# A new order table for a gated recurrence and an FFT gate on one core

## The chip, the core and the metric

The kernel runs on one core of one Trainium2 chip. The core has five engines that run side by side, each with its own queue of instructions in a fixed order: TensorE (PE in the profile, with its weight loads as PEld), VectorE (DVE), ScalarE (ACT), GpSimd (POOL) and SyncE (SP), which issues all DMA transfers of this kernel. The metric is the device time of one execution in microseconds (us), lower is better.

## The reference, cut to what matters

For four batches of 6272 tokens with 256 channels, a gated recurrence over time is followed by a gate with a convolution over the whole sequence, done by an FFT:

```
sig = 1 / (1 + exp(-f_logit))
f = lower_bound + (1 - lower_bound) * sig;  i = 1 - f
for t in range(S): h = f[:, t] * h + i[:, t] * x[:, t];  y[:, t] = h      # y is the next x
proj = x @ w_proj;  x1, x2, x3 = the three thirds of proj
x2_conv = irfft(rfft(x2, axis=1) * rfft(filter_fft, axis=0), axis=1)
out = (x1 * x2_conv * x3) @ w_out
```

## The kernel before

**The work of one batch**, in the names that the text uses (the operation's name in the program, its line in the profile):

- The recurrence goes in 13 chunks of 512 tokens (chunk 12 has 128). For a chunk, SP issues two loads of 512 KB (L331): the logit into FL and x into XT. `sig` is the sigmoid on ACT, in place in FL (L334). `u` multiplies XT by FL on POOL (L336). `su` turns FL and XT on PE into PSUM, once for each half of the channels, "a" and "b" (L348, 16 transposes each: eight of FL, eight of XT). `f` (L361 on ACT or L363 on DVE) and `scan` (DVE, L369) make the state, and `wrap` copies some of it (POOL L292, or ACT). FL and XT have three slots each, so the loads of chunk c wait until `su` b of chunk c-3 has read the slot. In batch 0 there are some slots more.
- Phase P (PE, L703) is the x2 projection, in 13 groups of which one is short; each is copied out of PSUM by ACT or DVE (`x2`, L280 or L285, tile X). It needs all scans of the batch. Then come the stages of the FFT: F1 (L716) with its copies, and 16 units of F2 (L778), of the product with the filter's spectrum (`prod`: DVE straight from PSUM, L801, or a copy by ACT or DVE and then `pm` on POOL, L810), of I2 (L820) and of the copy `Th`. A small product for each unit (`slot`, POOL L783) precedes I2. SP loads a unit's spectrum, H, from DRAM (L756), where the filter's stage at the start has stored it (`hst`, L660).
- `x13` (PE, L397) projects x1 and x3, and their product becomes zt (`xs`, `z`).
- Phase O has 13 groups: I1 (PE, L883), `y` (DVE, L889, tile ys, two buffers), `proj` (PE, L901), `o` (the copy out of PSUM, mostly ACT, L282 into osb, PP or HA) and `store` (SP, L913).

Phase O of one batch runs beside the recurrence of the next: while PE does I1 and proj of batch 0, it does `su` of batch 1 between them.

**The order.** Every operation is declared once, with its reads and writes, in a list (`Plan.op`); nothing is issued then. The string `ORDER` holds one word of three characters for each of the 2419 operations: the operation's number, its engine (with "MUL" for a product that DVE takes straight from PSUM), and for what PE writes, the PSUM bank. `emit` goes through the string and issues the operations in its order, and the waits between engines follow from the data. So the string fixes three things: each engine's queue (SP's too), who does an operation that two engines can do, and the PSUM banks, of which there are eight; most of PE's operations take a pair.

```
def order(self):
    ...
    for at in range(0, len(ORDER), 3):
        a, b, c = (value[d] for d in ORDER[at:at + 3])
        word = a * 4096 + b * 64 + c
        yield word // 64, self.ENGINES[word // 8 % 8], word % 8
```

An engine that comes to an operation whose data aren't there waits, with all that stands behind it in its queue. For SP that means that a load stands behind a store that waits for its copy.

Of the kernel before, what the change touches and what calls it, by code (L numbers as in the profile page):

```python
# [61 lines left out]
class Plan:  # L62
# [63 lines left out]
    "A3gA7gAzgA/gAAYAOYAVIA0YA4AAhQAcQABIACIAPIASYAQAAWIAjQAaQAbQAdQAfQAgQAeQA5QA1SAoUBAYAiUA2KA8ABHgBfgBPgAlUBBUArWAnWBD"  # L126
    "gBLgBXgBTgBbgBjgA9WAsSA6ABIYBJSBCMBEYAyAARAAYUAwVDqgDrgDngAkVD2gECgADgD3gDpgEOgDogEDgEPgEagAqVBQIA+OAXIBFQAmVBRWAuVB"
    "SGApVBGAAZEBKKBYIAUIBMYBNSATYBUYAxVBZWBgABOKBaOAtVBVQBWABcIAvUBhWBiOBdUBkYBeEBlQBmIBpUBqMBwQBxIBnWBoODsAD4ADtYEEAB3U"
    "BuQBvIBrYAEYByYBsWBtOB4EDuSBzQB+UB0AB5WD5YDyQB/EB6GCAUEQACBEDvKDwKB7YEFYCCYB8SDzID0ID6WB9CCDUCEED+QCJSCQUD/AEcAEmgD7"
    "OD8OERYEbgCKKCRMCOWEAIEngEygEGSCHUCIMCPGEHCEIKEoAEdYCLYCSYEKWCTQELGCMUCUACNEEMOESSCZQETKCXWE0AEWUCaICYGCeQCgWEUKE8gE"  # L130
    "zgAFgE9gFGgFQgCGgEpYEJYCbYEXMEYME+ACfAChGCcSCdCEeQEiWEjGEfIEgICnUCoECpSEqUEkOAIACqCCjQCwSCuWErECiYE1YAJYCkAEsMEuQFIA"
    "CvGCsUCxKE2SCzWEvIEwICtEC+UC0GE3KE4KE5QCrYAHYAKYCyYC/EE/YE6ADAWE7IDBGC3UFASC5WFSAC4EDDQC6GFDUDEAC8WC9GEhYFHgFbgF6gFJ"
    "YCVgFRgCmgC7YFTYDCYFagCFgFkgFlgB2gFugCWgDGgFvgAGgFcAFBKFCKFKSDJQJTWJUXFEMFFMFLKDKAJWHJVODOUDPEFmAFMKDHQFNWDIAJYUFOOF"
    "POJaEFUSDQQFVCDRADMUFWKFXWFdYDNEFwAFnYDLYEtYALYDSYAMYEVYElYFxYDXQFYOFZOFeSDYADTUFfCFhQDUEDZWFgKFiADaGFjIFoUFpEDeSDfC"
    "DgWDhGFrQFySDcWFqMJZUJdVFzKF0KF1SFsAMugB1gC2gF4gGlgG3gF/gDWgClgDFgMigMWgF5gC1gMXgD1YEBYExYJXYANYDxYD9YDbYF7YF8YDiYFt"
    "IF2KF3KDdGDjWJbsJeQJiRENAEZAJfFGHSGTUJkBJgoDkOGVQGJWGWIGICMwAGUEGKOGXSGFQGZUGYCGGIGaEMkAGBWGRSGDUGSCGLQGNSGCOMYAGEMG"
    "MIGOKGPUGQEJjWJnXJoQJluJpHJqoGbUDmgDlgHAgMjgDVgGugGdSGhWGcEGeKGfQGmUJsSGiGGgAGosGqsF9WJuCJtTHTgHJQJxSJvrF+GGjUJzCGvW"
    "GkMHKAG4SHLUG8CG6CGrYMZYGxuGzuGnYGwYGpYGsQG5YJyWJ2SJ3TG9YG0YG7YGyYGtAHMEG1QHBUG2AJ0uJ4KJ5rHFsHDsHPWHNQJ7TJ8SKAVHQGG+"
    "WKBUJ9DHOAJ+qHRQHUSKCNHSIG/GHYCMlYHWqKFVKGQKHFKIoKDsHVYHCYHGYHEYHHWHcgMvgGAgHlgHdSHfqHhqHIGHmQH3WHZYKEYHqAHXYHaUHgYH"
    "eYHrYHooHpYHiYHnYH4GHbEKKSKLRKMCKNBH5WHjUH7SH6OHvQHugIBgHkEH8CH9UH+EHsWHzoHxoICSHtGH/UIAMIEqIGCKPRMaWKRBJwYHwYH0YMxY"  # L140
    "JcYHyYKOYIFYILUMbGMeQIPEIHYIDYMcOMfAH1SKQVH2CMgIKStIKgINsITgIcgM6gIvgIlWImGIISIJCIdQIfAIUWIWGIYuIhAMmSMqUIQYIZYIVYIM"
    "YJmYIOYIXYI4gM7gNGgNHgJBgMrEMnKMsMMoKKUWKWGIRQKVXKZWISAKXvIaQIwUI0sIiYIgYIeYM8AM9YI1YMdYIbAKbGInSIpQKaXKeWKfVKcvIysI"
    "oCIqAIrSKjXKgGIsCKlPIjQKkUKhtIkAKmsItSI5WIuKNIAMyQM2UMzAI7uI9GM0INSgJKgKoSKpTKtWKuXNTgKqCKrrKnYIxYKJYJrYNJYJhYIzYM3E"
    "M4MM+QKvGKwHI2SM/ANCWI3CNAIJCUKySKzTNKQJGsNDGJEENegNEOK0CK1rNOUK3SNUANLAJ/YKsYK2YI+YI8YI6YKdYKxYKTYJHYJ6YKYYJFYNVYI/"
    "WK5CNPENMIJAGK4TK8SK9QLBRJLWK+CNgAJPGNQMK6rLDBNWUNaSNXELCRK/oLGQJNuNbCNYMNfgNogNpgLEpLIANqAJOYNzgNygLFYJ1YJMYJDYLAYN"
    "hYJQYKiYJIWLHQLJoJJGNiULLRLMQNlWNcKNjENkMJRSLOALNBNmGLQRLRQRyUJSCRzVLaSNnOLSBLToK7YNrYLKYLPYLUYLbKR0ER1FLVWNsQNvUNtA"
    "N0ANwELWOLcSNuILXWNxMLdCLkQLlILfSLYGLgKN9gN8gNRYNNYN1YNZYN+AN/YN2UN5WN3EN6GLmQLhSN4MN7OLuULvMOHgOGgLnALiCOIALpQOAWOD"
    "SLwULqILrQOECOFKOBGOCOL4SL5KLxELZgOQgLegLogORgLsAOSAOJYM5YM1YMhYMtYOKULzQONWObgOagLjgOTYNBYNFYOLEOOGL6SL7CL0IL1QL2AO"
    "MMOPOL9UL+MOUSOXQOVCR3WR4XOYAOcAL/UOWKOdYNdYOZIR5GR6HMpYOeSOhWU1gVBgL3gLygVOgVNgOfCOgKLtgOiGMAEMBgU2gVCgL8gMHQMCSOjO"
    "O4WU3AO5GMDKMIIOyUOmSOzEOnCO8QOuWO9IO2UOqQO3EOrIOkSO0UVDAOlCO1EOvOOwQOoSOxIOpCOsUVPAOtMO6QO7AMESMMUMNMMFCPAQPEWO+SPC"  # L150
    "UPBAO/KMJQMRSPFGPDEMGgMKAPIWMSKPGUPQSPHMPUCPoQPMuPKuMOUVEYU4YPNYPLYR2YR8XPJYR9TR+PPSqPpAPOQPYWPcuPauPdYPbYPTYPRYPVYM"
    "PER/DPPAPgUPsQPkEPtAPWSSBXSCVPZYR7YSDPSEtPisPlYPjYPhYSAYPXCPqQPrAPeSPuWPzQPfCPygP3oP1oMLgP7gQEgQNgPvGSGVSHUSIFSJEPmS"
    "P8WPnCPwUSLRSNBP+GU5SSMQPxMQAuSOoQBYP2YSKYP4YU6CQWUP0YP9YP/YP5WQXEU7KU9QP6GQFUQOSQJEU+IU/IQSCQCWQQqSQVSRTSSFSTrQaQSV"
    "VSWSQDGQHsSXNQIYQKYQGYQTYQRYQYWQbAQZGSaTQcQSbUSfWSgVScDSYqSZYShOSdsQdAQLSQeWQfOQggQpgQygQ7gVZgVagQhQSiFQMCQlAQjoVFUQ"
# [830 lines left out]
```

## Time and profile before

| what | value |
|---|---|
| median of 3 runs | 455.66 us (455.5 to 456.23) |
| the profiled execution's own time | 457.66 us |
| its span, first to last instruction | 455.5 us |
| busy PE, DVE, ACT, POOL | 96%, 90%, 86%, 68% of the span |
| granted TensorE clock | 0.998 |
| DMA | 119.04 MB, mean 261 GB/s |

The span is what the trace shows; 2.16 us of the profiled execution lie around it. A busy PE is not PE at its peak, because its matmuls overlap and their ends are modelled. In rows of the timeline the first number is the start in us, the second the length of the stretch, and brackets at the end give the engine's idle time before it and what ended that.

### The profile page before, as it was taken

The numbers are of one execution on the slowest core, as the hardware profiler recorded it, in microseconds if no ns is written. First come the engines' busy times: TensorE is split into PE (matmuls) and PEld (weight loads), VectorE is DVE, ScalarE is ACT, GpSimd is POOL, SyncE is SP. The second block draws the span as 40 slices with busy tenths as digits, with TensorE's granted clock in tenths as the row PEclk, the third lists the DMA queues.
The fourth block names the chain that finished last, engine by engine and source line by source line (L and its number), as shares of the span: only waits on it lengthen the run. The fifth ranks groups of instructions, "written<-read, shape, count | busy, mean of one in ns | idle before, by whom it ended". The sixth has DMA issues, their size and how long they took to land.

```text
span 455.5 us, 14537 instructions
## 1 busy us (share of the span) xinstructions
PE 436.8 (96%) x6017; PEld 344.1 (76%) x6017; DVE 407.9 (90%) x456; ACT 392.8 (86%) x545; POOL 307.6 (68%) x287
## 2 busy tenths in 40 slices
PE   8999999999999999999999999999999899999994
PEld 6877778667767889767768988776769797776783
DVE  5889998899999986999999987999999859988973
ACT  5789998889999988999988978999999778998354
POOL 4588994289998642889986626999996505657300
PEclk9999999999999999999999999999999999999999
DMA  8999979767797977559956893589586822763167
GB/s 326 406 402 380 373 254 362 275 217 242 273 322 237 333 250 316 173 172 325 357 195 232 308 358 146 179 293 339 192 309 210 349 115 89 219 199 111 47 266 302
DMA packets 42562, 119.04 MB, mean 261 GB/s; under 512 B 4096, under 2 KB 5760, under 8 KB 42496
## 3 DMA queue, kind: packets, MB, share of 16 engines
q1 hardware_dynamic: 42496, 118.11, 72.7%
q8 instruction: 47, 0.77, 0.7%
q14 instruction: 19, 0.16, 0.1%
HBM read 86.12 MB, written 31.98 MB: 259 GB/s over the span
## 4 chain that ended last, share of the span: by engine, by line
PE 58%; DVE 14%; ACT 8%; issue 5%; DMA 5%; POOL 3%; SPq 0%; DVEq 0%; ACTq 0%; POOLq 0%
PE PS L397 14%; PE PS L820 8%; PE PS L703 7%; PE PS L901 7%; DVE HA L369 6%; PE PS L348 6%; PE PS L716 5%; PE PS L778 5%; DMA FL<-in_f_logit_dram 3%; PE PS L883 3%; DVE ys L889 3%; DMA XT<-in_x_dram 2%; DVE fTs L363 2%; PE PS L633 2%; DVE PP L801 2%
## 5 line engine op out<-in xcount | busy, mean ns | idle before, releaser
L336 POOL TENSOR_TENSOR XT<-XT,FL 128x1024 f32<-128x1024 f32 (+1 forms) x47 | 105.1, 2239 | 59.5 <-ACT FL L334 31.7
L369 DVE TENSOR_TENSOR_SCAN HA<-fTs,HA,PS 128x512 f16<-128x512 f32 (+1 forms) x96 | 112.8, 1204 | 3.0 <-ACT fTs L361 2.2
L397 PE MATMUL PS<-HA,W 128*128 128x490 f16 (+1 forms) x416 | 100.4, 367 | 0.3 <-ACT XS L282 0.2
L810 POOL TENSOR_TENSOR PP<-HA,Hu 98x1008 f16<-98x1008 f16 x43 | 90.2, 2106 | 4.3 <-ACT HA L280 2.0
L280 ACT CAST HA<-PS 128x1024 f16<-128x1024 f32 (+1 forms) x106 | 83.5, 821 | 4.9 <-PE PS L716 1.8
L889 DVE TENSOR_TENSOR ys<-PS,zt 128x1024 fp32r<-128x1024 f32 (+1 forms) x52 | 58.5, 1153 | 9.7 <-PE PS L883 5.4
L801 DVE TENSOR_TENSOR PP<-PS,Hu 98x1008 f16<-98x1008 f32 x53 | 62.2, 1199 | 1.5 <-PE PS L820 0.7
L901 PE MATMUL PS<-Wo,ys 128*128 128x256 f32 x392 | 57.8, 293 | 3.3 <-DVE ys L889 2.6
L361 ACT ACTIVATE fTs<-PS,nomc 128x512 f32<-128x512 f32 (+1 forms) x84 | 55.8, 673 | 4.7 <-PE PS L348 2.3
L397 PEld LDWEIGHTS <-W 128*128 128x128 f16 x416 | 35.2, 97 | 29.9 <-issue 3.3
L820 PEld LDWEIGHTS <-PP 98*128 98x128 f16 x1024 | 48.9, 98 | 11.3 <-issue 2.9
L418 DVE TENSOR_TENSOR zt<-PS,XS 128x490 f16<-128x490 f32 (+1 forms) x86 | 54.7, 653 | 2.3 <-DVE XS L287 0.5
L282 ACT ACTIVATE XS<-PS 128x490 f32<-128x490 f32 (+1 forms) x85 | 49.0, 584 | 8.7 <-DVE zt L418 5.1
L901 PEld LDWEIGHTS PS<-Wo,ys 128*128 128x128 f32 x392 | 49.5, 188 | 8.3 <-ACT PP L282 1.5
L280 ACT CAST Th<-PS 128x784 f16<-128x784 f32 x63 | 51.7, 823 | 4.0 <-PE PS L820 3.3
L820 PE MATMUL PS<-VA,PP 98*128 98x98 f16 x512 | 52.0, 207 | 0.8 <-POOL PP L783 0.3
L820 PE MATMUL PS<-VB,PP 98*128 98x98 f16 x512 | 51.8, 207 | 0.0
L334 ACT ACTIVATE FL<-FL 128x1024 f32<-128x1024 f32 (+1 forms) x47 | 47.4, 1012 | 3.0 <-DMA FL<-in_f_logit_dram 2.8
L703 PE MATMUL PS<-W,HA 128*128 128x256 f16 x392 | 43.8, 273 | 0.0
L703 PEld LDWEIGHTS <-HA 128*128 128x128 f16 x392 | 42.8, 142 | 0.7 <-ACT XS L282 0.3
L348 PE MATMUL PS<-iden,FL 64*128 64x64 f32 x704 | 40.3, 230 | 2.7 <-ACT osb L282 1.4
L348 PEld LDWEIGHTS PS<-iden,FL 64*128 64x128 f32 x704 | 30.2, 138 | 15.1 <-DVE HA L369 3.4
(112 smaller groups left out, 764.8 us busy)
## 6 DMA issues: line engine op xcount, KB each, us to landing
FL<-in_f_logit_dram SPq DMA_DIRECT2D x43, 512.0 KB, 5.9
XT<-in_x_dram SPq DMA_DIRECT2D x43, 512.0 KB, 6.7
Hu<-H SPq DMA_DIRECT2D x39, 512.0 KB, 4.4
out_dram<-osb SPq DMA_DIRECT2D x24, 512.0 KB, 4.6
out_dram<-PP SPq DMA_DIRECT2D x16, 512.0 KB, 5.2
Hl<-H SPq DMA_DIRECT2D x13, 512.0 KB, 4.5
out_dram<-HA SPq DMA_DIRECT2D x8, 512.0 KB, 6.1
X<-in_moe_filter_fft_dram SPq DMA_DIRECT2D x7, 512.0 KB, 6.2
```

Of the source, the lines that this page charges most:

```text
L280: nc.scalar.copy(dst, src)
L336: op("u", {"POOL": 0.1 + 0.553 * nb}, lambda e, xt=xt, ft=ft: nc.gpsimd.tensor_tensor(xt, xt, ft, op=AOP.mult), r=[("ft", k)], w=[("xt", k)])
L348: nc.tensor.transpose(bank(pb)[:, at[p] + j:at[p] + hn:nb], src[ps, j, cols], iden[ps, ps])
L361: nc.scalar.activation(fT, sT, AF.Identity, scale=by, bias=1.0)
L369: nc.vector.tensor_tensor_scan(h, fT, bank(pb)[:, 512 - hn:512 + hn], init, op0=AOP.mult, op1=AOP.add),
L397: nc.tensor.matmul(PS[:, p, 0:n], W13[:, kh, js], HA[:, HB[kh] + t0:HB[kh] + t0 + n], start=(kh == 0), stop=(kh == 1))
L703: nc.tensor.matmul(pp[:, r - r0, :], column(HB[kh], q_of(r)), W2[:, kh, :], start=(kh == 0), stop=(kh == 1))
L801: nc.vector.tensor_tensor(pr, px.unsqueeze(1).broadcast_to([TB, 2, UE, 63]), hh(), op=AOP.mult)
L810: nc.gpsimd.tensor_tensor(pr, spec[:, o, :, 1:64].unsqueeze(1).broadcast_to([TB, 2, UE, 63]), hh(), op=AOP.mult)
L820: nc.tensor.matmul(PS[:, ib + o, pr * TB:(pr + 1) * TB], PP[:TB, k, o, n, 2 * pr:2 * pr + 2, :], v[:TB], start=(n == 0), stop=(n == 1))
L889: nc.vector.tensor_tensor(late["ys"][:, yk, :, 0:rn * 128], PS[:, cb:cb + 2, 0:rn * 128], late["zt"][:].rearrange("p k r m -> p k (r m)") ...
L901: nc.tensor.matmul(po[:, i, :], late["ys"][:, yk, kh, i * 128:(i + 1) * 128], Wo[:, kh, :], start=(kh == 0), stop=(kh == 1))
```

## The change

The string `ORDER` is replaced as a whole; nothing else in the program differs. The new string was searched with the loads of x and of the logit counted as landing later than the search had counted them, against the other transfers.

```
 ORDER = (
-    "A3gA7gAzgA/gAAYAOYAVIA0YA4AAhQAcQABIACIAPIASYAQAAWIAjQAaQAbQAdQAfQAgQAeQA5QA1SAoUBAYAiUA2KA8ABHgBfgBPgAlUBBUArWAnWBD"
...
+    "AzgAAYAOYA3gA0AABIAVYA4YACIAPIAhQAcQAjQAaQAbQAdQAfQA1QA5SAgUAeUAoUA/gBAYBBUA7gBHgAiWAlWBPgBXgBDgArWASIA2IA8YBIYDngBf"
...
```

Read word by word, the two strings hold the same 2419 operations. PE's 763 keep their number and kind, and 330 of them stand at another place in PE's queue, most by a few places. On SP 167 of 248 stand elsewhere. About 130 operations change their engine: ACT keeps 541, DVE goes from 437 to 431, POOL from 430 to 436 (many of POOL's and some of the others' issue nothing, where the product was taken from PSUM). The stretches of the queues that the prediction speaks of, before ("-") and after ("+"), with the batch ahead of the colon, fL and xL the loads of the logit and of x with their chunk:

```
SP, end of batch 1's recurrence
- 0:store0 1:fL11 0:store1 0:store3 1:xL11 1:xL12 1:fL12 0:store2
+ 0:store1 1:fL11 0:store0 1:xL11 1:fL12 0:store2 1:xL12 0:store3
ACT, the same place
- 1:f9b 1:f9a 0:o5 0:o4 1:sig11 1:f10a
+ 1:f9b 1:f9a 0:o5 1:sig11 0:o4 1:f10a
PE, batch 3's recurrence
- 3:su7b 2:proj1 3:su8a 2:I13 2:I14 2:proj2 2:proj3 2:I15 3:su8b 2:I16
+ 3:su7b 2:proj1 2:I13 3:su8a 2:I14 2:proj2 2:proj3 3:su8b 2:I15 2:I16
SP, start of batch 3's loads
- 1:store2 1:store5 1:store3 1:store6 3:fL1 1:store4 3:xL2 3:fL0 3:xL1 3:fL2 1:store7 3:xL0
+ 1:store2 1:store5 1:store4 3:fL0 3:fL1 3:fL2 1:store6 3:xL1 3:xL0 1:store3
PE, end of batch 3
- 3:I19 3:proj10 3:proj9 3:I111 3:I112 3:proj11 3:proj12
+ 3:I19 3:proj10 3:I112 3:I111 3:proj9 3:proj11 3:proj12
POOL, the last units of batch 3 (what issues)
- slot13 pm27 slot12 pm26 slot14 pm28 pm30 pm31 slot15
+ z13 slot13 pm26 slot12 pm24 slot15 pm31 pm30 pm28 slot14 z23
PE, the same place
- 3:I214 3:x1348 3:I215 3:x1349 3:x1350 2:proj11
+ 3:x1345 3:x1346 3:x1347 3:x1348 3:x1349 3:x1350 3:I214 2:proj11
PE and ACT, phase P of batch 0
- PE P3 P9 P10 P4 P11 P2 P12 P0 P8 P1 P5 P6 P7
+ PE P12 P10 P5 P0 P3 P1 P8 P4 P6 P2 P7 P11 P9
- ACT x23 1:sig2 x29 x211 x212 1:sig1 x28 1:sig0 x27
+ ACT 1:sig2 xs6 x212 1:sig0 x210 x20 x23 x28 1:sig1 x24 x26 x22 x29
SP ahead of that phase
- 1:fL2 hst0 hst9 H0 H2 hst13 hst6 hst10 1:fL1 1:fL0 hst8 1:xL0
+ hst10 hst11 1:xL2 1:fL2 hst2 hst5 1:fL0 hst6 1:fL1 hst7 hst12 hst15 hst14 hst13 H0
```

In batch 0, too, two `wrap` copies (wrap5, wrap7) go from ACT to POOL, where all twelve then stand ahead of phase P.

More of the change, by code (lines that the diff above doesn't have):

```diff
@@ L130 @@
[L130 to L154, printed above, removed]
@@ L185 @@
[L185 to L188 removed]
+    "AzgAAYAOYA3gA0AABIAVYA4YACIAPIAhQAcQAjQAaQAbQAdQAfQA1QA5SAgUAeUAoUA/gBAYBBUA7gBHgAiWAlWBPgBXgBDgArWASIA2IA8YBIYDngBf"
@@ L189 @@
+    "Qk4Ok0Sk5Wk1Ck9IlGSk2glCMk+Qk6GlDUlQWk/AlEElHKlISlROlJClLQlaUlMIlSSlNWlTClbMlVQlOGlkUk7glWIlcSlXQlAglFglUglKglPgllMl"
+    "fWlmUldClYAlgOluQlpSlhWlqKlnElrUlZglvIlwQloglxIliGlegljglsEltglyg"
 )
```

98 lines of the change are left out of this document (60 added, 38 removed).

## The prediction

> **What bounds the kernel now.** I read the page first, then the waits grouped by who waited for whom, then the chain that ended last, and then the timeline of each engine around the few places where PE stood idle.
>
> ```profile
> span 455.5 us, 14537 instructions
> PE 436.8 (96%) x6017; PEld 344.1 (76%) x6017; DVE 407.9 (90%) x456; ACT 392.8 (86%) x545; POOL 307.6 (68%) x287
> ...
> POOL XT L336 <- DMA XT<-in_x_dram: 27.6, 5, 12.6
> ...
> SPq L331 <- PE PS L348: 110.0, 40, 10.0
> ```
>
> PE is busy for 436.8 of 455.5 us, and the change leaves its work as it is: the same matmuls in the same shapes, of which 433 of 763 operations keep their place. So a new order can win only what PE stands idle, 18.7 us with the head and the tail, and it can lose by making new idle time. The other two lines say where loads matter. SP waits 110.0 us for the transposes (`su`) that free a slot; this is the ring of three at work and costs nothing by itself. POOL's 27.6 us for x are no loss either, as long as POOL, at 68%, isn't what PE waits for. A late load costs only where PE is reached in the end. Four of PE's longest idle times are these:
>
> ```profile
> 162.26 0.46 PE L348 MATMUL PS<-iden,XT 64*128 64x64 f32 x8 [0.70 <-POOL XT L336]
> ...
> 278.20 1.20 PE L901 MATMUL PS<-Wo,ys 128*128 128x256 f32 x8 [0.51 <-ACT X L280]
> ...
> 358.92 0.46 PE L348 MATMUL PS<-iden,FL 64*128 64x64 f32 x8 [1.39 <-ACT osb L282]
> ...
> 449.30 1.42 PE L901 MATMUL PS<-Wo,ys 128*128 128x256 f32 x10 [1.36 <-DVE ys L889]
> ```
>
> The first three have a load behind them, as the next rows show; the fourth is the tail, where no load is left. They are 0.70 + 0.51 + 1.39 + 1.36 = 3.96 us together, and that is the size of what can be had here.
>
> **The change part by part.** *One: chunk 11 of batch 1.*
>
> ```profile
> 149.49 0.45 SPq L913 DMA_DIRECT2D out_dram<-osb  x1
> 151.52 0.34 SPq L913 DMA_DIRECT2D out_dram<-PP  x1
> 151.96 2.13 SPq L331 DMA_DIRECT2D XT<-in_x_dram  x2
> ...
> 151.96 7.70 DMA XT<-in_x_dram
> ...
> 155.06 2.10 ACT L282 ACTIVATE HA<-PS 128x1024 f32<-128x1024 f32 x2
> 157.06 1.05 ACT L334 ACTIVATE FL<-FL 128x1024 f32<-128x1024 f32 x1
> ...
> 159.82 2.38 POOL L336 TENSOR_TENSOR XT<-XT,FL 128x1024 f32<-128x1024 f32 x1 [1.59 <-DMA XT<-in_x_dram]
> ```
>
> The load of x stands in SP's queue behind two stores, and the second waits for its copy out of PSUM until 151.5. The load goes out at 151.96, lands 7.70 us later, and POOL, idle for 1.59 us, multiplies until 162.2, when PE waits 0.70 us. In the new table one store stands ahead (store0, copied by then) and store3 behind, so the load can follow the store at 149.49, at about 149.94: 2.0 us earlier, and with one store of 512 KB less ahead of it. ACT's `sig` also moves ahead of one of the two copies at 155.06, by 2.10 / 2 = 1.05 us. Sig would end near 157.1, x land near 157.7 even at an unchanged 7.70, and POOL begin 2.1 us earlier than 159.82. PE needs it at 162.26 - 0.70 = 161.56 at the earliest; POOL would be done near 160.1. The wait goes: **-0.70**. What is late next is the scan ahead of phase P, on DVE, which also starts earlier.
>
> *Two: chunk 11 of batch 3.*
>
> ```profile
> 348.84 0.62 PE L883 MATMUL PS<-ID,Th 64*128 64x128 f16 x16
> 349.31 0.41 PE L348 MATMUL PS<-iden,FL 64*128 64x64 f32 x8
> ...
> 349.79 7.08 DMA FL<-in_f_logit_dram
> ...
> 356.90 1.06 ACT L334 ACTIVATE FL<-FL 128x1024 f32<-128x1024 f32 x1 [1.95 <-DMA FL<-in_f_logit_dram]
> 357.86 1.92 ACT L282 ACTIVATE osb<-PS 128x1024 f32<-128x1024 f32 x2
> ```
>
> This is a chain of queues: `su` 8b on PE frees the slot, the logit's load goes out and lands 7.08 us later, ACT has stood still 1.95 us for it, and the two copies behind that sigmoid hold the PSUM banks that PE's next `su` needs. The new table puts su 8b ahead of one I1, that is by 349.31 - 348.84 = 0.47 us; ACT's queue here still has the sigmoid ahead of the two copies. So **-0.47** of the 1.39.
>
> *Three: the first logits for batch 3, during phase P of batch 2.*
>
> ```profile
> 263.86 0.34 SPq L331 DMA_DIRECT2D XT<-in_x_dram  x1
> ...
> 264.77 0.59 SPq L331 DMA_DIRECT2D XT<-in_x_dram  x1
> ...
> 265.47 8.79 DMA FL<-in_f_logit_dram
> ...
> 274.33 1.06 ACT L334 ACTIVATE FL<-FL 128x1024 f32<-128x1024 f32 x1 [0.69 <-DMA FL<-in_f_logit_dram]
> ```
>
> Two loads of x and a store stand between the logits on SP, and ACT waits 0.69 us for the last one with copies out of phase P behind it; PE then waits the 0.51 us. The new table issues the three logits one after the other, with x behind. Two transfers fewer ahead is well over 0.69 us. **-0.51**, from both sides: nothing if the copies are late for another reason, and not more than the row.
>
> *Four: the tail.*
>
> ```profile
> 446.09 1.18 PE L901 MATMUL PS<-Wo,ys 128*128 128x256 f32 x8 [0.33 <-DVE ys L889]
> 447.20 0.74 PE L883 MATMUL PS<-ID,Th 64*128 64x128 f16 x20
> 447.92 1.56 DVE L889 TENSOR_TENSOR ys<-PS,zt 128x1024 fp32r<-128x1024 f32 x2 [1.98 <-PE PS L883]
> ```
>
> Before, proj9 waits 0.33 us, then the last two I1 run, then y11 begins at 447.92. After, the two I1 come first: 0.74 us from 446.09 - 0.33 = 445.76 to 446.50, then proj9 for 1.18 until 447.7, and y11, which needs the buffer that proj9 reads, begins there: **-0.2**.
>
> *Five: the head.*
>
> ```profile
> 69.85 1.17 POOL L292 COPY HA<-HA 128x512 f16<-128x512 f16 x2
> ...
> 70.13 1.13 ACT L280 COPY HA<-HA 128x512 f16<-128x512 f16 x2
> 71.97 10.88 PE L703 MATMUL PS<-W,HA 128*128 128x256 f16 x98
> ```
>
> Phase P starts at 71.97, and POOL's last copies for it end at 71.02. ACT's two copies move to POOL, about 1.17 us more: 72.2, past the cover of 0.95 by **+0.2**. Behind them on POOL stands the clearing of the buffer into which phase P is copied, which shifts alike. A gain here is excluded as long as that string is the last; a loss could be larger if POOL, which also gets three more of the early copies, starts it later.
>
> The other moves I cost at nothing: 130 changes of engine, which nearly balance (ACT 541 operations both times, DVE 437 to 431), beside a PE that is busy all the while; their bounds are in the range. **The sum** is -0.70 - 0.47 - 0.51 - 0.2 + 0.2 = -1.7 us. The profiled execution would go from its own 457.66 to 456.0, and the median, 2.0 below it, from 455.66 to **454.0**. If the second and fourth wait went wholly, 0.92 + 1.16 more would go: 451.9.
>
> Against this speaks the Trainium skill, "DMA: Bandwidth & Descriptors", section "Anatomy of one DMA": a transfer is put at about 2.0 us plus its bytes at 436 GB/s, for 512 KB an estimate of 3.2 us. By that, no load here would be late and the first three terms would be zero, a sum of 0.0 and no change. The trace doesn't agree where it matters: 7.70, 7.08 and 8.79 us in the rows above, with other transfers ahead.
>
> **The rivals.** *(S) Phase P of batch 0 is held by a sigmoid.*
>
> ```profile
> 67.65 0.46 PE L348 MATMUL PS<-iden,FL 64*128 64x64 f32 x8
> 70.38 1.53 SPq L331 DMA_DIRECT2D FL<-in_f_logit_dram  x2
> ...
> 78.79 1.06 ACT L334 ACTIVATE FL<-FL 128x1024 f32<-128x1024 f32 x1
> ...
> 82.89 1.01 ACT L280 CAST X<-PS 128x1024 f16<-128x1024 f32 x1 [1.18 <-PE PS L703]
> ```
>
> The new table puts sig0 of batch 1 on ACT ahead of all but one of its copies out of phase P; before, most copies went first, and ACT began the logit's sigmoid at 78.79, 8.4 us after the load went out. That load now leaves when su 11b has read the slot, near 68.1. PE takes 10.88 / 98 = 0.111 us for a matmul; a short group and five long ones, 42 matmuls, bring it to 76.6, and the next group (P8) needs the bank that ACT frees by x210, behind sig0. With 1.06 for the sigmoid and 1.01 for the copy, the logit must have landed by 74.6, within 6.5 us. If it takes 8.4, it lands at 76.5, x210 ends at 78.6, PE stands 2.0 us, and ACT has eight copies and one more sigmoid from 77.6 on: 86.7, against 83.9 for the last copy before. That is +2.8, and 454.0 + 2.8 = **456.8**, slower. For it: the DMA engines are full in the head. Against it: in the new SP queue less stands ahead of this load (the spectra H come after it), so some 6 us or less are likelier.
>
> *(G) The gain is given back by POOL at the end of batch 3.*
>
> ```profile
> 413.72 2.10 POOL L810 TENSOR_TENSOR PP<-HA,Hu 98x1008 f16<-98x1008 f16 x1
> ...
> 415.99 2.10 POOL L810 TENSOR_TENSOR PP<-HA,Hu 98x1008 f16<-98x1008 f16 x1
> ...
> 418.73 6.22 POOL L810 TENSOR_TENSOR PP<-HA,Hu 98x1008 f16<-98x1008 f16 x3
> ...
> 426.84 0.93 PE PS L901 x8
> ```
>
> Five products as before, but the one for I2 of unit 14 is now the last of them, and that I2 stands right ahead of the proj that began at 426.84, so it is due near 426.1. If the string of five starts at 413.7, it ends at 413.7 + 5 x 2.1 + some 1.0 of small products = 425.2, in time. If its first copy comes as late as the second product did, 415.99, it ends at 427.5, 1.4 late, and everything after it shifts: 454.0 + 1.4 = **455.4**, no change that can be told.
>
> *(N) The change does nothing.* If the three waits had another cause than the place of the loads, because a load lands when the transfers let it and not sooner for an earlier issue, terms one to three would be zero, and -0.2 and +0.2 leave **455.7**. For it: the load of x took 7.70 us with two stores ahead, and stores move the same bytes wherever they stand. Against it: 7.70, 7.08 and 8.79 us differ from place to place, and the longest has the most ahead of it. The rule of the Trainium skill quoted above ("DMA: Bandwidth & Descriptors") would give this time too.
>
> **How the numbers follow.** A measurement of this kernel can tell about 0.2%, 0.9 us, from no change. The forecast, 454.0 with a range of its own from 452.3 to 455.2, gets 0.50 (0.45 faster, 0.05 within 0.2%). S gets 0.20, all slower. G gets 0.16, half within 0.2% and half slower, since its price has no firm upper end. N gets 0.04, the same. The remaining 0.10 is for moves that I did not cost, 0.02 faster and 0.08 slower. So 0.47 faster, 0.17 the same, 0.36 slower. The range goes from 452.2, with most of the second and fourth wait gone, to 457.4, which takes in S and a little more.
>
> **What would show it.** Right: the load of x at the end of batch 1's recurrence goes out within 0.5 us of the logit's neighbour store, and PE's wait for POOL there is gone; the wait of 1.39 for `osb` is near 0.9; ACT's wait for a logit in phase P of batch 2 is gone; y11 starts when proj9 ends. Wrong: ACT idle on FL in phase P of batch 0 with PE waiting for X behind it (S), PE waiting for PP from POOL ahead of the last I1 (G), or a phase P that starts over 0.5 us later than 71.97. If PE's idle time has fallen and the span has not, its busy time has grown, and my reading of the idle rows as the whole of the slack is wrong.

## The result, and the profile after

The new table is slower: median 458.06 us (456.65 to 460.03, 12 runs) against 456.0 us (455.04 to 458.08, 12 runs) of the kernel before beside it, a ratio of 1.0036 with a 95% interval of 1.0021 to 1.0052. The forecast was 454.0. The profiled execution of the new table took 459.92 us, its span is 457.7. First the page, and the two waits that were shown of before:

```profile
span 457.7 us, 14559 instructions
PE 439.2 (96%) x6017; PEld 345.0 (75%) x6017; DVE 403.3 (88%) x452; ACT 395.9 (86%) x547; POOL 310.6 (68%) x289
...
POOL XT L336 <- DMA XT<-in_x_dram: 15.0, 2, 11.8
...
SPq L331 <- PE PS L348: 131.3, 41, 8.7
```

Loads of x are indeed less in the way: POOL waits for them 15.0 us in two places where it was 27.6 in five. PE's busy time is 439.2 instead of 436.8, at a mean granted clock of 0.993 against 0.998: phase P of batch 3 alone ran at 0.93 in this execution and took 11.66 us instead of 10.93. Up to the first F1 of batch 0 PE is busy for 80.38 us where it was 80.37, in 85.91 us instead of 84.00, so what is lost there is idle time. Next the timeline at the four places that the prediction counted on:

```profile
151.40 0.38 SPq L913 DMA_DIRECT2D out_dram<-osb  x1
151.88 0.38 SPq L331 DMA_DIRECT2D XT<-in_x_dram  x1
...
159.05 2.38 POOL L336 TENSOR_TENSOR XT<-XT,FL 128x1024 f32<-128x1024 f32 x1 [0.53 <-ACT FL L334]
...
270.69 1.06 ACT L334 ACTIVATE FL<-FL 128x1024 f32<-128x1024 f32 x1 [0.58 <-DMA FL<-in_f_logit_dram]
...
282.17 1.21 PE L901 MATMUL PS<-Wo,ys 128*128 128x256 f32 x8
...
358.78 0.46 PE L348 MATMUL PS<-iden,FL 64*128 64x64 f32 x8 [0.18 <-ACT osb L282]
...
449.81 1.56 DVE L889 TENSOR_TENSOR ys<-PS,zt 128x1024 fp32r<-128x1024 f32 x2 [1.72 <-PE PS L901]
...
451.18 1.42 PE L901 MATMUL PS<-Wo,ys 128*128 128x256 f32 x10 [1.47 <-DVE ys L889]
```

Chunk 11's load of x goes out right behind one store, and POOL waits for the sigmoid, no longer for x. The proj at 282.17 has no bracket, where one of 0.51 us stood, but ACT still waits for a logit in phase P of batch 2, 0.58 us where it was 0.69. The 1.39 us ahead of `su` is 0.18. The last y (in the row of two from 449.81) starts when proj9 ends. But for that wait of ACT each step is there as described, and the kernel is slower.

Most of the loss stands in the first 30 us. The filter's rows come in 13 loads; `fr` casts four rows (POOL L292, DVE L285 or ACT) into afs, which has two buffers, `rot` rotates them on PE (L618), and a copy of each goes to tile f. FF1 (L633) needs all 13. FTr is a small table made by two multiplications. Before:

```profile
16.08 1.04 POOL L292 CAST afs<-X 128x1024 fp32r<-128x1024 f32 x1 [0.92 <-PE PS L618]
17.59 0.63 DVE L287 TENSOR_SCALAR FTr<-HA,cols 128x196 fp32r<-128x196 f32 x2
21.75 0.40 POOL L292 CAST afs<-HA 128x256 fp32r<-128x256 f32 x1 [2.09 <-PE PS L618]
23.43 2.88 PE L633 MATMUL PS<-D1r,f 128*128 128x256 f32 x20 [0.84 <-DVE f L285]
28.93 1.22 DVE L369 TENSOR_TENSOR_SCAN HA<-fTs,PS 128x512 f16<-128x512 f32 x1
...
71.44 0.48 DVE L369 TENSOR_TENSOR_SCAN HA<-fTs,HA,PS 128x128 f16<-128x128 f32 x1
```

After:

```profile
17.20 1.04 POOL L292 CAST afs<-X 128x1024 fp32r<-128x1024 f32 x1 [1.73 <-DMA X<-in_moe_filter_fft_dram]
18.30 0.74 PE L618 MATMUL PS<-afs,rot 128*128 128x256 f32 x4 [1.14 <-POOL afs L292]
21.17 1.78 POOL L294 TENSOR_SCALAR FTr<-HA,cols 128x196 fp32r<-128x196 f32 x2
22.91 0.39 POOL L292 CAST afs<-HA 128x256 fp32r<-128x256 f32 x1
24.60 2.29 PE L633 MATMUL PS<-D1r,f 128*128 128x256 f32 x16 [0.41 <-DVE f L285]
28.82 0.69 DVE L285 CAST afs<-PS 128x512 fp32r<-128x512 f32 x1
30.29 1.22 DVE L369 TENSOR_TENSOR_SCAN HA<-fTs,PS 128x512 f16<-128x512 f32 x1
...
73.34 0.48 DVE L369 TENSOR_TENSOR_SCAN HA<-fTs,HA,PS 128x128 f16<-128x128 f32 x1
73.88 10.88 PE L703 MATMUL PS<-W,HA 128*128 128x256 f16 x98
```

Three things push one chain. The cast of rows 24 to 27 starts at 17.20 instead of 16.08 and waits for its load, not for PE. The last cast stands behind FTr, 1.78 us on POOL where DVE took 0.63, and starts at 22.91 instead of 21.75. So the first FF1 starts at 24.60 instead of 23.43. Then one FF1 more stands ahead of the first transposes, and DVE copies its result (28.82) ahead of the first gate: the first scan starts at 30.29 instead of 28.93. From there to phase P DVE hardly stands still: between the first scan's start and the last scan's end it is busy for 42.28 of 42.99 us before and for 42.62 of 43.53 after. So the 1.36 us at the first scan stay, and another 0.54 come with the other copies that the new table puts between the scans (0.34 us more work, 0.20 more idle). Phase P starts at 73.88 instead of 71.97, and the first F1 of batch 0 at 85.91 us instead of 84.00.

### The profile page after: what moved, and what is told of

It reads as the page before. It is cut to its first block, busy times and chain, and to the rows that moved or that the text cites. A ratio compares the mean times of both kernels' runs of the same rounds, so it can differ in the third digit from the quotient of the medians.

```text
span 457.7 us, 14559 instructions
## 1 busy us (share of the span) xinstructions
PE 439.2 (96%) x6017; PEld 345.0 (75%) x6017; DVE 403.3 (88%) x452; ACT 395.9 (86%) x547; POOL 310.6 (68%) x289
## 4 chain that ended last, share of the span: by engine, by line
PE 56%; DVE 19%; DMA 8%; ACT 7%; issue 5%; SPq 2%; POOL 2%; DVEq 0%; ACTq 0%; POOLq 0%
PE PS L397 14%; DVE HA L369 9%; PE PS L820 8%; PE PS L901 7%; PE PS L778 6%; PE PS L348 5%; PE PS L703 5%; PE PS L716 5%; DVE ys L889 4%; DMA X<-in_moe_filter_fft_dram 3%; PE PS L883 3%; PE PS L633 2%; DMA out_dram<-PP 2%; DMA FL<-in_f_logit_dram 2%; DMA H<-HA 1%
## 5 line engine op out<-in xcount | busy, mean ns | idle before, releaser
L810 POOL TENSOR_TENSOR PP<-HA,Hu 98x1008 f16<-98x1008 f16 x42 | 88.2, 2106 | 3.7 <-ACT HA L280 2.9
L801 DVE TENSOR_TENSOR PP<-PS,Hu 98x1008 f16<-98x1008 f32 x54 | 63.5, 1199 | 1.5 <-PE PS L820 0.6
L361 ACT ACTIVATE fTs<-PS,nomc 128x512 f32<-128x512 f32 (+1 forms) x86 | 57.0, 671 | 3.8 <-PE PS L348 1.9
L282 ACT ACTIVATE XS<-PS 128x490 f32<-128x490 f32 (+1 forms) x88 | 51.3, 584 | 5.7 <-PE PS L397 4.6
L703 PE MATMUL PS<-W,HA 128*128 128x256 f16 x392 | 44.8, 276 | 0.1
L348 PE MATMUL PS<-iden,FL 64*128 64x64 f32 x704 | 40.3, 230 | 1.6 <-ACT PP L282 0.6
L280 ACT CAST X<-PS 128x1024 f16<-128x1024 f32 (+1 forms) x31 | 30.9, 1074 | 11.4 <-PE PS L703 11.2
```

Of the source, the lines that this page charges most:

```text
L280: nc.scalar.copy(dst, src)
L348: nc.tensor.transpose(bank(pb)[:, at[p] + j:at[p] + hn:nb], src[ps, j, cols], iden[ps, ps])
L361: nc.scalar.activation(fT, sT, AF.Identity, scale=by, bias=1.0)
L703: nc.tensor.matmul(pp[:, r - r0, :], column(HB[kh], q_of(r)), W2[:, kh, :], start=(kh == 0), stop=(kh == 1))
L801: nc.vector.tensor_tensor(pr, px.unsqueeze(1).broadcast_to([TB, 2, UE, 63]), hh(), op=AOP.mult)
L810: nc.gpsimd.tensor_tensor(pr, spec[:, o, :, 1:64].unsqueeze(1).broadcast_to([TB, 2, UE, 63]), hh(), op=AOP.mult)
```

## The experiments

The unit of every edit is a word of the order string, so edits are given as queues. In the kernels of the first four runs every line number is two lower (L346 for L348). A ratio stands for the time against the kernel before on the same chip, with its 95% interval.

**FTr back on DVE.** In the queues `idw`, `rest` and the like make other small tables, and `u0` is the first product of the recurrence.

```
- POOL fr8 fr11 FTr fr12 u0       DVE idw0 fr10 rest1
+ POOL fr8 fr11 fr12 u0           DVE idw0 FTr fr10 rest1
```

> The new table with one operation changed: the two multiplications that make the table FTr (1.78 us on POOL in the profile after, 0.63 us on DVE in the one before) go back to DVE, into its idle stretch of 2.83 us before 21.09 us. Theory H (the head lost it: POOL's FTr holds the last cast of the filter, which holds the last rotation, which holds the first FF1): that cast starts at 22.3 instead of 22.91 us, as soon as the rotation ahead has read its buffer; the first FF1 starts 0.6 us earlier than 24.60, near 24.0; the transposes of chunk 0 start near 28.0 instead of 28.64; the time falls by 0.6 us, a ratio to the kernel before near 1.002. Rival D (the head's loss is made by the scans' start and by DMA, not by POOL): first FF1 within 0.1 us of 24.60, ratio 1.0036. Rival P (DVE is late in turn with its next copy out of PSUM): first FF1 at 24.6 or later.

Measured: 1.0008 (0.9991 to 1.0025), 1.3 us less than the new table's 1.0036; the two intervals just overlap.

```profile
16.67 1.05 POOL L290 CAST afs<-X 128x1024 fp32r<-128x1024 f32 x1 [0.92 <-PE PS L616]
21.84 0.40 POOL L290 CAST afs<-HA 128x256 fp32r<-128x256 f32 x1 [1.17 <-PE PS L616]
23.56 2.29 PE L631 MATMUL PS<-D1r,f 128*128 128x256 f32 x16 [0.41 <-DVE f L283]
```

The last cast waits for PE again and not for POOL's own queue. Theory H holds, but the profile has more than it foresaw: the first FF1 is 1.04 earlier and not 0.6. In this execution the load of rows 24 to 27 happened to land at 16.29 us; in six other executions with the new order's loads (the new table's and those of runs further down) it landed at 17.03 to 17.36. So two causes are mixed in the 1.04. Those six part them: with FTr on POOL the first FF1 starts at 24.60 to 24.89 (three executions, mean 24.75), with FTr on DVE at 24.05 to 24.39 (three, mean 24.25). FTr is worth 0.5 us there, near the 0.6 of theory H, and the landing of the load the rest. The last section of runs takes up the load.

**Old head, new rest, joined at phase P of batch 0; and new head, old rest.** The edit is one cut in the list of operations: all that one order has issued by then, then what is left in the other's order.

> The order of before for every operation up to the first matmul of phase P of batch 0, then the new order for all the rest. Theory H: the head's 1.9 us are gone and the rest keeps its own gains and losses: phase P of batch 0 starts near 72.0 us instead of 73.9, the time falls by about 1.9 us against the new table, to a ratio between 0.997 and 1.000 to the kernel before. Rival L (the loss lies in the later parts, and the late head would have been taken up by waits there): ratio near 1.0036 although phase P starts at 72.0.

> The new order up to the first matmul of phase P of batch 0, then the order of before for all the rest. Theory H: phase P starts near 73.9 us instead of 72.0 and everything behind it shifts alike: 1.9 us more than before, a ratio near 1.004. Rival L (later waits take the head's delay up): ratio below 1.002.

The new head with the old rest: 1.0036 (1.0018 to 1.0053), the whole loss of the change. The first F1 of batch 0 starts at 86.17 us. Nothing behind the head takes the delay up, and Rival L falls. The old head with the new rest gave 1.0176 (1.0147 to 1.0205), which neither theory had:

```profile
80.72 1.06 ACT L332 ACTIVATE FL<-FL 128x1024 f32<-128x1024 f32 x1 [5.20 <-DMA FL<-in_f_logit_dram]
...
82.73 8.81 PE L701 MATMUL PS<-W,HA 128*128 128x256 f16 x56 [5.24 <-ACT X L278]
```

The old head sends batch 1's logit late, and the new order asks for its sigmoid early: PE stands 5.24 us behind ACT. This is rival S of the prediction, made by the joint; in the changed kernel itself it did not occur. So this run can't show what the rest is worth.

**The last logit of batch 3.** In the new table this load stands behind a store:

```
- SP 3:xL11 2:store2 2:store4 3:xL12 2:store3 3:fL12
+ SP 3:xL11 2:store2 2:store4 3:fL12 3:xL12 2:store3
```

> The new table with the load of the logit's last chunk of batch 3 ahead of the load of x and of one store on SP, as it stood before the change; nothing else moved. Theory F (this load, put behind a store that waits for its copy, is what gave back the gain at the end of batch 3): ACT no longer waits 1.23 us for it, POOL's last product there starts near 362.9 instead of 364.10, PE's waits of 0.52 and 0.41 us ahead of phase P of batch 3 fall to 0.2 together; the time falls by 0.7 to 1.0 us, a ratio near 1.0018. Rival C (the loss of 1.3 us at the start of that phase P in the profile after came from the granted clock, 0.76 there, and the two waits overlap with DVE's scans anyway): ratio within 0.0006 of 1.0036.

First the new table, then this run:

```profile
356.17 0.69 SPq L331 DMA_DIRECT2D FL<-in_f_logit_dram  x1
363.60 0.42 ACT L334 ACTIVATE FL<-FL 128x256 f32<-128x256 f32 x1 [1.23 <-DMA FL<-in_f_logit_dram]
364.10 0.72 POOL L336 TENSOR_TENSOR XT<-XT,FL 128x256 f32<-128x256 f32 x1 [2.99 <-ACT FL L334]
364.88 0.28 PE L348 MATMUL PS<-iden,XT 64*128 64x64 f32 x2 [0.52 <-POOL XT L336]
```

```profile
364.21 0.41 ACT L332 ACTIVATE FL<-FL 128x256 f32<-128x256 f32 x1
366.10 0.25 PE L346 MATMUL PS<-iden,XT 64*128 64x64 f32 x2
```

The wait for the load is gone, and from `su` 11b to 12b it is 3.53 us instead of 4.58. But the time is 1.0029 (1.0014 to 1.0045), within the noise of 1.0036. The mechanism of theory F is shown; the gain in time of this run alone is not.

**More mending of the head, and an earlier joint.** FF14 is number 4 of FF1, FF20 number 0 of FF2 (PE L651), the filter's second stage; `afs5` copies an FF1 out of PSUM, `hw` an FF2.

```
- PE FF20 FF14 FF15 su0a FF21      DVE hw0 afs5 f0a scan0a      ACT afs4 sig2
+ PE FF20 su0a FF14 FF15 FF21      DVE hw0 f0a scan0a           ACT afs4 afs5 sig2
```

> The new table with three edits in the head: FTr on DVE as in the run before this one (its transposes of chunk 0 stood at 27.59 us instead of 28.64), the transposes of chunk 0 ahead of two FF1 on PE instead of behind them, and the copy of one of these FF1 on ACT instead of on DVE ahead of the first gate. Theory H (the rest of the head's loss is the one FF1 more ahead of the first transposes, 0.6 us): the first scan starts near 28.5 us (before 28.93, new table 30.29), phase P of batch 0 near 72.0 instead of 73.9, and the time falls by 1.9 us against the new table: ratio to before 0.999 to 1.0005. Rival D (DVE's string of scans is then held by something else, a later logit or x): first scan near 28.5, but phase P at 72.5 or later, ratio 1.001 to 1.002.

> The order of before up to the first transposes of chunk 2 of batch 0 (34.7 us), the new order from there. The earlier joint at phase P brought 5.2 us of waiting for a logit of batch 1 on ACT, since the old head sends that load late and the new order asks for its sigmoid early; here the loads of chunks 3 and up go out in the new order. Theory H: the first scan at 28.9 as before, phase P of batch 0 at 72.0 to 72.4, ratio 0.999 to 1.0005, as for the mended head. Rival L (the new order of the middle of the head has a loss of its own): phase P at 73 or later, ratio 1.002 or more.

Both missed: 1.0049 (1.0030 to 1.0068) and 1.0072 (1.0051 to 1.0093). With the first the transposes of chunk 0 stand at 27.41 us, but those of chunk 1 at 33.65, later than in the new table (32.82): PE waits for ACT's copies, which moved back with the one added. With the second the joint makes PE wait 1.63 us for a scan. Neither tells the theories apart; each is a new order with a fault of its own.

**The four terms alone, on the old order.** These are only the moves that the prediction names, one by one: xL11 of batch 1 ahead of store3, sig11 ahead of o4, su8b of batch 3 ahead of I15, the three logits of batch 3 together, and the two I1 of the tail ahead of proj9. The rest of the queues stays as before, but for five PSUM banks; in the new table more stands elsewhere (su8a of batch 3 behind I13, for one).

> The order of before, with only the four edits that the prediction gave a gain: the load of x for chunk 11 of batch 1 ahead of store3 and its sigmoid ahead of a copy; transposes 8b of batch 3 ahead of an I1; the three logits of batch 3 one after the other in phase P of batch 2; the last two I1 ahead of proj9. Theory T (the prediction's terms are true): 1.9 us less, ratio 0.996. Theory V (the waits of 0.51 and 1.39 us belonged to the one profiled execution and not to the kernel: with the old order behind the new head neither was there): at most the 0.7 and the 0.2 are won, ratio 0.998 to 1.000. Rival U (each wait taken away is met again at the next link of the chain): ratio 1.000.

Measured 1.0054 (1.0033 to 1.0076): slower, where the prediction's terms give 0.996. The trace says term by term why. Chunk 11 of batch 1: the wait for x is gone, but PE waits 0.79 us for the copy that the sigmoid was moved ahead of. The three logits: the stretch from the end of batch 2's recurrence to its first mini falls from 18.94 to 18.37 (mini is PE L732, a short matmul ahead of a batch's F2). Transposes 8b of batch 3:

```profile
349.20 0.63 PE L883 MATMUL PS<-ID,Th 64*128 64x128 f16 x16 [0.25 <-DVE ys L889]
349.86 1.22 DVE L889 TENSOR_TENSOR ys<-PS,zt 128x1024 fp32r<-128x1024 f32 x1 [0.72 <-PE PS L883]
351.14 0.63 PE L883 MATMUL PS<-ID,Th 64*128 64x128 f16 x16 [1.31 <-DVE ys L889]
```

The I1 that `su` 8b was moved ahead of feeds DVE's y, DVE now waits 0.72 us for it, and the next I1 waits 1.31 us for the bank that y reads. In the traces of the new table and of its tail end on other heads PE has no such wait there, so this link belongs to the edit alone. The tail: PE waits 0.63 us ahead of an I1 for a copy that the new table has in another order and this kernel doesn't; that part of the run is a fault of the edit.

**The kernel before, profiled again.**

> The kernel before, unchanged, profiled a second time. Theory V (the waits of 0.70, 0.51 and 1.39 us on which the first three terms rest vary from execution to execution with the landing of loads): at least one of the three is shorter by half here, and the rest is not. If they belong to the kernel, all three are within 0.15 us of the first profile.

> The kernel before against itself, timed as the others are. Ratio 1.000, with an interval of 0.0015 to either side: that is what a difference has to exceed. The wait of 1.39 us at the end of batch 3's recurrence: 0.3 us, as in the second profile, or 1.3, as in the first; the span behind it follows.

Against itself it gives 1.0000 (0.9981 to 1.0018); the other was executed once, in 459.65 us at a granted clock of 0.948, and isn't compared in time. Of the 1.39 us that was the largest gap behind the prediction, the two profiles show:

```profile
358.12 1.06 ACT L334 ACTIVATE FL<-FL 128x1024 f32<-128x1024 f32 x1 [0.86 <-DMA FL<-in_f_logit_dram]
360.14 0.46 PE L348 MATMUL PS<-iden,FL 64*128 64x64 f32 x8 [0.30 <-ACT osb L282]
```

```profile
356.44 1.06 ACT L334 ACTIVATE FL<-FL 128x1024 f32<-128x1024 f32 x1
358.84 0.43 PE L348 MATMUL PS<-iden,FL 64*128 64x64 f32 x8
```

0.30 in one and nothing in the other, where ACT doesn't wait for the logit at all. The 0.70 is 0.52 in the first and absent in the second; the 0.51 is 0.40 and 0.56. Theory V holds for the 0.70 and the 1.39, while the 0.51 comes back. The same load took 7.08, 6.04 and 5.80 us to land in the three executions, and ACT's wait for it is 1.95, 0.86 and 0. The first profile, at 457.66 us with a median of 456.0 beside it, had caught the longest wait of the three.

**Joints at 165 us and in the tail, FTr and a cast to POOL, and a first combination.** At the end of batch 1's recurrence and at the tail's start both orders have issued exactly the same operations.

```
- POOL fr8 fr12      ACT f24 fr11      DVE fr9 FTr f26
+ POOL fr8 fr11 FTr fr12
```

> The order of before with two operations moved to POOL in the head, as in the new table: the cast of the filter's rows 44 to 47 (from ACT) and the two multiplications for FTr (from DVE), both ahead of the last cast. Theory H (POOL's string ahead of the last cast makes the head late): on POOL 1.04 us from 19.65, 1.78 us from 20.7, last cast at 22.4 instead of 21.75, first FF1 near 24.0 instead of 23.43, phase P of batch 0 0.6 us later, ratio 1.0013. Rival: DVE, relieved of 0.63 us, and ACT, of 1.06, bring the rotations' copies earlier by as much, ratio 1.000.

> The two orders joined where they have issued the same operations, at the end of batch 1's recurrence (165 us of the profile before): the order of before up to there, the new one behind. It holds terms two, three and four of the prediction in their full surroundings, and neither the head nor term one. Prediction's terms: -0.47 - 0.51 - 0.2 = -1.2 us, ratio 0.9975. Theory V (term two's wait of 1.39 us was an event of one execution, 0.30 us in the second profile of before, and the last logit of batch 3, which now stands behind a store, costs 0.9 us ahead of phase P): three and four gain 0.5 and 0.4, the logit takes 0.9: ratio 1.000. Rival W (the new second half is slower by itself): 1.002 or more.

> The order of before up to the first proj of batch 3 (430.5 us), where both orders have issued the same operations, and the new one for the tail. Term four: the last y starts when proj9 ends, 0.2 us earlier by the prediction, 0.4 by the shift between the two profiles from that proj to the last: ratio 0.9991 to 0.9996. Rival: the PE wait of 1.36 us ahead of proj11 only grows by as much, ratio 1.000.

> A version made of the parts that the profiles so far show to gain: the new order with FTr on DVE up to the end of batch 1's recurrence (0.2 to 0.25 us earlier there than before, with term one in it), the order of before from there with the three logits in phase P of batch 2 one after the other (0.55 us in the profile of the four terms), and the new tail (0.4). Sum -1.2 us, ratio 0.9974. If the head's remaining 0.6 us isn't won back by term one: ratio 0.999.

The two operations moved to POOL in the old head: 1.0011 (0.9995 to 1.0028), first FF1 at 23.59. The last cast starts at 21.96, not at 22.4: POOL stood idle 2.09 us there before, which takes up FTr's 1.71. So in this trace FTr on POOL costs nothing without a chain that is late already; the time, whose interval holds both 1.0000 and theory H's 1.0013, can't tell. The three joined orders gave 1.0031 (1.0017 to 1.0045), 1.0017 (1.0002 to 1.0033) and 1.0056 (1.0036 to 1.0077), all worse than expected. Their traces have waits at the joints that no other trace has: in the combination 1.51 us on an I1 behind the copy of a PSUM bank, in the tail 1.37 us. The two orders give the same holder different banks there. They were joined again with the second order's banks renamed:

> The order of before up to the end of batch 1's recurrence, the new one from there, as in the earlier run of this joint, but with the new order's PSUM banks renamed so that each holder at the joint has the same bank on both sides: the joint then makes no wait (in the earlier run phase P of batch 1 was 1.5 us longer than in any other). Theory S (over all the executions profiled so far, the new order's pieces behind 165 us are, against the old one's: -0.1, -0.1, -0.6, +0.6, +0.6, -0.1, 0.0 us): ratio 1.0000 to 1.0010, so no gain from terms two, three and four together. The prediction's terms: 0.9975.

> The new order with FTr on DVE up to the end of batch 1's recurrence, then the order of before with the three logits one after the other in phase P of batch 2, its banks renamed to fit at the joint; the tail as before. By the pieces: head +0.3, term one -0.6, the middle as before, the logits -0.6: -0.9 us, ratio 0.998. If the logits' gain is given back behind them: 0.9993.

Old head with new rest: 0.9992 (0.9974 to 1.0010). So behind the head the new table gains 0.4 us, give or take 0.8, of the 1.2 that terms two to four promised there; with the new head's 1.0036 the account closes within the intervals. The combination: 0.9989 (0.9970 to 1.0009), half of the 0.9 us that were expected, with the whole inside the interval.

**One term alone, and the two last causes.**

> The order of before with term three alone: in phase P of batch 2 the three logits' loads go out one after the other, ahead of the loads of x and the store that stood between them. Prediction's term: -0.51 us, ratio 0.9989; from the end of the recurrence to the first mini of batch 2 18.37 us as in the run of the four terms, where before had 18.37 to 19.53 in five executions. If the loads of x, now later, are met as a wait at the first transposes of batch 3: 1.000.

The three logits alone: 0.9992 (0.9976 to 1.0008). The stretch is 18.36 us in this trace and 18.35 to 18.37 in all four executions with this edit, against 18.37 to 19.53 (mean 18.99) in six without. Of the 0.62, the next stretch gives 0.30 back (67.20 against 66.90 on the mean), since the loads of x go out later.

```
- SP ff4 pre0 ff11 ff6 ff8          (on the combination; ff6 loads rows 24 to 27)
+ SP ff4 ff6 pre0 ff11 ff8
```

`pre0` issues nothing, so the load goes ahead of one load, ff11.

> The combined version of the run before (new order with FTr on DVE up to the end of batch 1's recurrence, then the old order with the three logits one after the other), with one more edit: the load of the filter's rows 24 to 27 goes out one place earlier on SP, ahead of two other loads. Theory H2 (the head's loss has two causes, FTr on POOL and this load): it lands near 14.7 instead of 17.3 us, the rotation that needs it starts at 17.6 instead of 18.3 to 18.6, the first FF1 at 23.5 instead of 24.3, the first F1 of batch 0 at 84.6 instead of 85.4; ratio 0.997 to 0.998 (0.9989 without the edit). Rival: the rotations behind wait for another load in turn, first FF1 at 24.0 or later, ratio 0.9989.

> The order of before up to the end of batch 1's recurrence, the new one from there with its banks renamed, and the load of the logit's last chunk of batch 3 ahead of x and a store, as it stood before the change. Theory F: from the transposes 11b to 12b of batch 3 3.5 us, where the new order had 3.5 to 4.7 in six executions (mean 4.2); 0.6 us less than the run without this edit (0.9992), ratio 0.998. Rival: the store that now goes out later holds a buffer, or the wait moves to the scans: ratio 0.9992.

The filter's load one place earlier, on the combination: 455.62 us median, 0.9978 (0.9960 to 0.9996). It is the fastest kernel here, 0.2% under the kernel before and 0.6% under the new table. Its only trace is of an execution of 1035.45 us and shows nothing of this. The interval also overlaps with the combination's, so that the load won the last 0.0011 is not shown. The old head and new rest with the logit early: 0.9988 (0.9973 to 1.0003), with 3.18 us from `su` 11b to 12b, so the wait is gone; the time is 0.2 us less than without, where 0.6 was expected, and that is within the noise.

## Why the prediction was wrong, step by step

The forecast was off by 3.3 us: -1.7 was predicted, and +1.6 came. About 1.5 of it is the head (term five), and the other 1.8 is that the four gains together came to next to nothing. Seventeen of the profiled executions hold stretches of the old or of the new order undisturbed. The table gives, for each stretch between the starts of two operations on PE, the mean, the range and the number of executions of either kind. Each stretch begins where the one above it ends.

| stretch | old order, us | new order, us | difference |
|---|---|---|---|
| start to first mini, batch 0 | 89.30 (88.81-90.07, 8) | 91.02 (90.87-91.16, 2) | +1.72 |
| to `su` 10b, batch 1 | 68.94 (68.80-69.48, 10) | 69.02 (68.76-69.80, 7) | +0.08 |
| to `su` 12b, batch 1 (term one) | 7.26 (6.88-7.85, 10) | 7.07 (6.70-7.58, 7) | -0.19 |
| to `su` 12b, batch 2 | 98.34 (97.72-99.38, 7) | 98.05 (97.87-98.86, 7) | -0.29 |
| to first mini, batch 2 (term three) | 18.99 (18.37-19.53, 6) | 18.91 (18.57-19.45, 8) | -0.08 |
| to `su` 8b, batch 3 (term two) | 66.90 (66.65-67.19, 6) | 66.40 (66.11-66.79, 8) | -0.50 |
| to `su` 11b, batch 3 | 10.97 (10.42-11.82, 9) | 11.65 (11.12-12.62, 8) | +0.68 |
| to `su` 12b, batch 3 | 3.51 (3.50-3.58, 9) | 4.17 (3.52-4.68, 6) | +0.66 |
| to first proj, batch 3 | 66.00 (65.85-66.74, 9) | 65.68 (65.18-67.09, 8) | -0.32 |
| to last proj (term four) | 19.89 (19.79-20.16, 7) | 19.53 (19.52-19.54, 8) | -0.36 |
| to the end | 5.14 (5.12-5.20, 7) | 5.38 (5.29-5.52, 8) | +0.24 |

The differences sum to +1.64 us; measured were 0.36% of 456.0, or 1.64 as well. That they agree to the last digit is luck: one of the old executions is the one at a clock of 0.948, and without it no difference moves by more than 0.12, but the sum is +1.97. Behind the head the differences sum to -0.08, where terms one to four promised -1.88; the run that joins the old head to the new rest gave -0.4, give or take 0.8. The -0.29 and the -0.32 were not traced to any move.

**Term five, the head, is the step that failed.** It was sized at +0.2 from POOL's last copies ahead of phase P, and it is +1.72. The prediction looked at the end of POOL's string. What sets phase P is DVE's chain of 26 scans with the gates and copies between them, in which DVE is idle for less than 1 us; so whatever starts the first scan later counts in full, some 50 us ahead of the rows that were read, and whatever else is put between the scans counts too. That the loss is the head's is shown by the joined runs (the new order up to phase P of batch 0 gives 1.0036, the new order behind batch 1's recurrence 0.9992). How it divides among FTr, the load, the one FF1 more and the copies between the scans is read off the traces; of these only FTr was moved alone in the new table, for 1.3 us. The text did say that three more early copies go to POOL and could start it later, and did not price it, though the rows for that were in the profile of before: FTr 0.63 us on DVE, no row for it on POOL, and the nearest one there a cast at 1.04. It did name the sign, a phase P over 0.5 us later than 71.97: it starts at 73.88. The Trainium skill, "GPSIMD Engine Reference", section "Engine selection", puts operations with one input on GpSimd at roughly line rate beside VectorE. The trace disagrees for this one: 1.78 us for the pair on POOL against 0.63 on DVE, 2.8 times as long. For the plain casts of 128x1024 it is nearer the rule, 1.04 on POOL against 0.68 to 1.08 on DVE in the two traces.

**Term one** (-0.70) is -0.19 on the mean. The wait for x is there in five of ten executions of the old order, 0.44 to 0.90 us, and in three of seven of the new (0.48 to 0.77), there at chunk 12. The wait comes and goes with the landing of the load, in either order; the table shows no gain beyond that.

**Term two** (-0.47) moved `su` 8b ahead by the length that was read, -0.50, but that alone is no gain. The I1 that it passes takes 0.46 us ahead of `su` 8b in the old order and 0.45 us behind it in the new, so it only changes sides of the mark, and the next stretch has it: +0.68. The two stretches together are +0.18. The wait that was to shrink, of `su` 10a for the copy into osb, stands in three of nine executions of the old order (0.30 to 1.39 us) and, over 0.15 us, in five of eight of the new (0.18 to 1.46), so it wasn't won either. The prediction counted when the load goes out and left out that PE has to do the I1 later, and whoever waits for that I1 with it, which the run of the four terms shows.

**Term three** (-0.51) is right taken alone, -0.62 in its stretch, of which 0.30 comes back behind it. In the new table the stretch gains only 0.08; ACT still waits there for a logit (0.58 us in the profile after), the groups of phase P stand in another order, and which of these takes the gain wasn't tried.

**Term four** (-0.2) is -0.36 at the last proj and +0.24 behind it, -0.12 together. Before, then after:

```profile
450.75 0.42 DVE L287 TENSOR_SCALAR osb<-PS 128x256 f32<-128x256 f32 x1 [1.27 <-PE PS L901]
```

```profile
453.02 0.42 DVE L287 TENSOR_SCALAR osb<-PS 128x256 f32<-128x256 f32 x1 [1.65 <-DMA out_dram<-osb]
```

The last copy used to wait for its proj and now waits for a store to leave its buffer. The reordered stores of the tail were in the diff and not in the sum.

**What the sum lacked**: the last logit of batch 3, behind a store in the new queue of SP, +0.66 on the mean (four of six executions have it, two have 3.52 and 3.53 us as before). It stands six places behind the load that term two is about.

**The base of the sum** was wrong too. All terms were taken off one execution of 457.66 us, and the distance of 2.0 us to the median was carried along as if it were constant; but the wait of 1.39 us, of which two further executions have 0.30 and nothing, can itself be much of that distance.

**The rivals**: S did not occur in the changed kernel (from phase P's start to the first F1 of batch 0 it is 12.03 us in both traces), G neither (between the last F2 of batch 3 and the first I1 PE has no wait over 0.15 us in the new trace, which is 1.86 us behind the old at the one and 2.15 at the other). N, that the loads' places change nothing, is nearest to what the rest of the kernel did, though term three alone speaks against it. The rule of the Trainium skill that the prediction set against itself ("DMA: Bandwidth & Descriptors", section "Anatomy of one DMA") is given there for transfers that GpSimd issues, while SP issues all of them here. In the trace of before the first load, with none ahead of it, took 3.79 us against that rule's estimate of 3.2, and the ninth 10.1. The case that came is the one that had no price, "moves that I did not cost", with 0.08 for slower; term five had named its direction.

## What to carry to other kernels

Ahead of a chain that has no gap up to a point where everything waits for its end, find what starts it, and price every move there, even of a 0.6 us operation to an engine with slack on the mean. A wait of a load that one profile shows is a sample: profile the kernel two or three times before taking it off the time, and count only what recurs. When an operation is moved ahead of another, the cost is with whoever waits for the other, and what is gained at one link is only worth what the next link leaves of it. And when a mark on the time line is itself what was moved, read the gain at a later mark, behind all that it passed.

## What the runs showed of the hardware

One place further back in a full queue can cost a load more than the length of one load. The loads of the filter land 1.28 us apart (512 KB each; for tile X, before: 13.45 and 14.73), and the load that went from the ninth place to the tenth landed at 17.06 instead of 14.73:

```profile
DMA to landing us min/median/max: 5.4/7.0/10.1
```

```profile
DMA to landing us min/median/max: 5.4/7.0/11.3
```

These are the rows for tile X before and after; the maximum is that load. Of the 2.33 us the place explains 1.28; the rest is that one step along the queue is longer in each of nineteen traces, 2.05 to 2.70 us. With the old order of loads it comes at the eleventh or the twelfth load (twelve executions), with the new one at the tenth in six of seven, and two loads later in the run with FTr on DVE. Why it comes earlier stays open. And two orders that are sound by themselves lose 1.4 to 5.2 us at a joint where they disagree on the PSUM bank of one holder, or on how early a load was sent.
